# Two more feature tiles made and turned in the spatial stage of a one-core gMLP and linear-attention kernel

## The chip, the cores and the metric

The kernel runs on one core of a Trainium2 chip. Its engines are TensorE (PE, with its weight loads as PEld), VectorE (DVE), ScalarE (ACT), GpSimd (POOL) and the sync engine (SP), each with an instruction queue of its own. The time is device microseconds of one execution. Some runs are profiled: one execution with start and duration of each instruction.

## The reference

All is f32, S = 2048 rows, D = 512. The normalized input goes through two branches, which are added to x.

```python
xn = layernorm(x)
# branch A: 32 heads of 16, hedgehog features, linear attention
q, k, v = split(xn @ wqkv)
phi = concat(softmax(h @ w_phi), softmax(-h @ w_phi))     # for q and for k, per head
num = phi_q @ (phi_k.T @ v)
den = phi_q @ sum(phi_k) + 1e-6
A = (num / den) @ wo
# branch B: gMLP, Fh = 688
z = gelu(xn @ w_in);  z1 = z[:, :688];  z2 = layernorm(z[:, 688:])
g = w_sp @ z2 + b_sp[:, None]                             # w_sp is 2048 x 2048
B = (z1 * g) @ w_out
out = x + A + B
```

## The kernel before

Rows are handled in 16 tiles of 128. Products that need f32 accuracy are done with operands split in two, a part rounded to the PE's format and the remainder: `mm3` (lines 55 to 59) issues three matmuls for each, rounded by rounded (L57), rounded by remainder (L58), remainder by rounded (L59). ACT rounds (L49), DVE subtracts to get the remainder (L53).

The stages follow one another on PE. First come layer norm and the projections to k, v and q; the exponentials of the 16 tiles of q features and the reciprocals of their softmax sums go to DRAM as `e_d`. Then come the projections z1 (raw to DRAM, `z_d`) and z2 (gelu, layer norm, split into the B operands).

The **spatial stage** computes g = w_sp @ z2 for eight pairs of row tiles. It does so with the seven products P1 to P7 of a 2 x 2 scheme of Strassen's kind (`FORM`), whose A operands are A11, A22 and sums S1 to S4 of quarters of w_sp. A pair has four units (quarters of the columns); unit n is 42 matmuls on g. For each unit `load_a` fetches a raw tile wf on SP, and `prep_a` makes the operands: ACT rounds A11/A12, A22, S2/S1, S4/S3, and DVE makes four sums (L637 to L640) and four remainders (L53, `A<-wf,A`). This is done two units ahead, into two sets of tiles in turn. The raw tiles wf lie in a ring of three (f, x, y).

After a pair's last unit, DVE and ACT **drain** the seven products from PSUM into tile c (one ACT copy, seven DVE instructions, L834 to L840). Then `gate` multiplies: POOL has loaded the pair's z1 into tile z1t (L808), ACT takes its gelu (L850), DVE multiplies it with c (L853), and `turn` transposes the result in blocks of 32 on DVE (L862, L864) back into z1t. From there stores on SP bring it to DRAM in turned order (`u_d`, `ur_d`). Tiles c and z1t have one buffer each.

**Features** of q still need the denominator: `q_fin` (L563 to L570) multiplies with `zb`, the sums of phi_k, reduces, and scales; its operands are the tile's e and r from `e_d`. Tiles 0 and 1 are finished so before the spatial stage and stored back. After pairs 2 and 4 they are loaded into tile c by POOL (L967), turned by DVE (`turn_q`, L579) into tile z1t, and stored by POOL as `q_d` (L581). Tile 2 is finished at the end of the spatial stage, tiles 3 to 15 in the final stage (`features`).

The **final stage** goes over pairs of row tiles: `project_u` multiplies u with w_out, `attend` the turned features with kvT (po, L1062), `project_o` with wo. Features reach `attend` turned in two ways (`attend_T`): tile pair 0 and tiles from TQ = 8 on come from `q_d`; tiles 2 to 7 are transposed on PE (ptq, L1047) and copied by ACT. `ahead(i)` loads e of tile i + 5 and finishes tile i + 3.

The order on each engine is set by a scheduler, which places instructions by a timeline of its own and keeps each engine's queue in that order. At the border between the z2 projections and the spatial stage the function `in_turn` fixes, by a list of keys, the order of preparations, B splits and drain steps on DVE (first instruction of a key) and ACT (second).

Of the kernel before, what the change touches and what calls it, by code (L numbers as in the profile page):

```python
# [10 lines left out]
F32 = mybir.dt.float32  # L11
# [7 lines left out]
P = 128  # L19
# [22 lines left out]
def mixer(ctx: ExitStack, tc: tile.TileContext, x, x_t, wv, wqkT, phi_bd, wo, w_in, wst, b_r, w_out, out):  # L42
# [509 lines left out]

    QW = NF + 7 * H

    def load_q(s, et):
        sp.dma_start(et[:, :NF + 2 * H], e_d[s])
        return et

    def q_fin(et, tmp, zb):
# [40 lines left out]

    def load_a(n):
        i, q = SEQ[n]
        tag = "fx"[n] if n < 2 else "fxy"[(n - 2) % 3]
        t = (fy[0] if tag == "y" else ws).tile([P, 2, QC, P], F32, tag="wf" + tag, name="wf")
        for k in range(2):
            with tc.issue_after(load_a.last) if n == 5 else ExitStack():
                load_a.last = sp.dma_start(t[:, k], wst[2 * i + k, :, q * QC:(q + 1) * QC, :]).ins
        return [t[:, k].rearrange("p (k two) t -> p two k t", two=2) for k in range(2)]
# [37 lines left out]

    def in_turn(*keys):
        for e in range(2):
            queue = [turns[k][e] for k in keys if e < len(turns[k])]
            for a, b in zip(queue, queue[1:]):  # L650
                tc.add_manual_dep(b, a.name, mybir.DependencyInfo(
                    mybir.DependencyClass.NoSync, mybir.DependencyReason.DATA), reason="order of the border")
# [177 lines left out]
    def drain(i, g, cb):  # L830
        g = {k: t[:, :FC] for k, t in g.items()}
        b1, b2 = (bias[:, 2 * i + k:2 * i + k + 1] for k in range(2))
        c11, c12, c21, c22 = (cb[:, k, j] for k in range(2) for j in range(2))
        add = lambda o, p, b, q: dve.scalar_tensor_tensor(o, p, b, q, op0=ALU.add, op1=ALU.add)  # L834
        first = act.activation(c12, g["P1"], AF.Copy)
        steps = [add(c11, g["P2"], b1, c12),
                 dve.tensor_tensor(c21, g["P6"], c12, op=ALU.add),
                 dve.tensor_tensor(c12, g["P5"], c21, op=ALU.add),
                 add(c22, g["P7"], b2, c12),
                 dve.tensor_tensor(c21, g["P7"], c21, op=ALU.add),  # L840
                 add(c12, g["P3"], b1, c12)]
        drained = add(c21, g["P4"], b2, c21)
        for k, x in enumerate(steps + [drained]):
            turns["c", i, k] = x.ins,
        return cb, first.ins, drained.ins

    def gate(i, cb, z, u, ut, after=None):
        cb, first, _ = cb
        with tc.issue_after(after or first):
            act.activation(z[:, :, :FH], z[:, :, :FH], AF.Gelu_apprx_tanh)  # L850
        zs = z[:, :, :FH].rearrange("p k (j f) -> p k j f", j=2)
        us = u[:, :, :FH].rearrange("p k (j f) -> p k j f", j=2)
        dve.tensor_tensor(us, zs, cb, op=ALU.mult)  # L853
        lo, hi = u[:, :, KF * P:FH], u[:, :, FH:FU].bitcast(F32R)
        dve.tensor_copy(hi, lo)
        rest_l(lo, lo, hi)

        def turn():
            src = ut.rearrange("p k f -> p (k f)")
            m, r = src[:, :2 * KF * P], src[:, 2 * KF * P:]  # L860
            for k in range(2):
                dve.transpose(m[:, k * KF * P:(k + 1) * KF * P].rearrange("p (m c t) -> p m c t", c=KF, t=BL),  # L862
                              u[:, k, :KF * P].rearrange("p (c m j) -> p m c j", c=KF, j=BL))
            dve.transpose(r.rearrange("p (k f) -> p k f", k=2), u[:, :, KF * P:])  # L864
            eng = pool if i == NP - 2 else sp
            for b in range(0, P, BL):
                w = b // BL * KF * BL
                eng.dma_start(u_d[2 * i:2 * i + 2, :, w:w + KF * BL].rearrange("k (m j) w -> j (k m) w", j=BL),
                              m[b:b + BL].rearrange("p (m w) -> p m w", w=KF * BL))
                eng.dma_start(ur_d[2 * i:2 * i + 2, :, b:b + BL].rearrange("k (a j) t -> j (k a) t", j=BL),  # L870
                              r[b:b + BL].rearrange("p (a t) -> p a t", t=BL))

        return turn
# [44 lines left out]
    for n in range(NC):  # L918
        i = SEQ[n][0]
        if n % NQ == 1 and i < NP - 1:  # L920
            z = load_z1(i)
        if n:
            products(n, g)
        if n % NQ == NQ - 1 and i < NP - 1:
            c = gt.tile([P, 2, FU], F32, tag="c", name="c")
            cq = c[:, :, :FH].rearrange("p k (j f) -> p k j f", j=2)
            cb = drain(i, g, cq)
            g = {}
        if n + 4 < NC:
            raw[n + 4] = load_a(n + 4)  # L930
        if 0 < n < NC - 2:
            A[n + 2] = prep_a(n + 2, raw.pop(n + 2))
        if n == 6:
            in_turn((1, "sums"),
# [24 lines left out]
        if n % NQ == NQ - 1 and i < NP - 1:  # L959
            turn = gate(i, cb, z, c, z, prep_a.last)  # L960
            if i < NP - 2:
                turn()
            if i in (2, 4):
                s = i // 2 - 1
                e, t = (gt.tile([P, 2, FU], F32, tag=tag, name=name).rearrange("p k f -> p (k f)")[:, :NF]
                        for tag, name in (("c", "c"), ("z1", "z1t")))
                pool.dma_start(e, e_d[s, :, :NF])  # L967
                turn_q(s, t, e, pool)
        if n == NC - 4:
            stage_w()  # L970
        if n == NC - 3:
            zb = slot("zb")[:, :NF]
            sp.dma_start(zb, zb_d)
            uT = [first_gate(0)]
            ets[2] = load_q(2, slot("et"))
            es[2], last = q_fin(ets.pop(2), slot("qtmp")[:, :NF], zb)
        if n == NC - 2:
            fq = [slot("f")[:, :NF].rearrange("p (k b c t) -> p k b c t", k=2, c=NB // 2, t=BL) for h in range(2)]
            for k in range(2):
                for h in range(2):  # L980
                    sp.dma_start(fq[h][:, k], q_d[k].rearrange("p (b h w) -> h p b w", h=2, w=QB // 2)[h])
            t = xz_tile((KF + 1) * P, F32R, "u1")
            us = {1: load_u(1, t[:, :KF * P].bitcast(F32), t[:2 * REM, KF * P:(KF + 1) * P])}
    cb = drain(NP - 1, g, slot("c").rearrange("p (k j f) -> p k j f", k=2, j=2))
    with tc.issue_after(cb[2]):
        turn()
# [134 lines left out]
            rows = [(m * QP, (m + 1) * QP) for m in range(c // 2 * 8 + c % 2, (c // 2 + 1) * 8, 2)]  # L1121
            load_w(wo, rows, wo_h[:, c], wo_l[:, c], cw.tile([P, D], F32, tag="wof", bufs=4, name="wof"))
    with tc.issue_after(load_w.last):
        ets[3] = load_q(3, slot("et"))
        for s in (2, 3):
            us[s] = fetch_u(s)
        ets[4] = load_q(4, slot("et"))

    def ahead(i):

        if i + 5 < NT:
            ets[i + 5] = load_q(i + 5, slot("et"))
        if i + 4 < NT:
            with tc.issue_after(brought[i + 2]) if i + 6 >= NT else ExitStack():
                us[i + 4] = fetch_u(i + 4)
        if 3 < i + 3 < NT:
            features(i + 3)

    p, nxt = {}, dict(enumerate(uT))
    for i in range(0, NT, 2):  # L1140
# [10 lines left out]
            p[i + 1] = project_u(i + 1, u, q)  # L1151
        if not i:
            fin.append(lasts[7])
            features(3)
            with tc.issue_after(fin[-1]), tc.issue_after(lasts[8]):
                nxt[2] = gated(us.pop(2))
        if i < NT - 2:
# [48 lines left out]
```

## Time and profile before

| | us |
|---|---|
| median of 3 runs | 610.74 |
| lowest and highest | 610.21, 615.73 |
| profiled execution | 612.24 |
| its span, first to last instruction | 610.5 |
| granted PE clock | 1.000 |
| spatial stage, first g matmul to first pout matmul | 275.4 to 484.3 |

Times in the profile count from the start of the span. A row of a timeline gives start, length, engine, line, operation, what it writes and reads, how many instructions are merged and, in brackets, how long the engine stood idle before and what ended that. A row of the groups gives busy time and mean length in ns, then idle time before and its releasers. A row of waits gives who waited for whom: total, times, longest. The chain of waits is followed back from the last instruction. A releaser with a DMA's name is inferred from a semaphore that several transfers share, so the name can be that of another transfer.

### The profile page before, as it was taken

The page shows a single profiled execution, that of the slowest core. Times are in us where ns is not written, and L with a number is a line of the kernel's source. Part 1 is how long each engine was busy: PE and PEld are TensorE (multiplying, and loading weights), DVE is VectorE, ACT ScalarE, POOL GpSimd, SP SyncE. Part 2 cuts the span into 40 slices and gives each one's busy share as a digit, 9 for nine tenths or more (in the row PEclk, how much of TensorE's full clock was granted, in tenths as well). Part 3 has the DMA queues.
Part 4 walks back from the last instruction along what each step waited for, and adds up shares of the span by engine and source line. Part 5 has one row for each costly group of instructions (what it writes and reads, how often), then busy time and mean ns, then how long its engine had stood idle before and what let it go on. Part 6 is the DMA issues. An engine that isn't in the chain of part 4 may idle for free.

```text
span 610.5 us, 11382 instructions
## 1 busy us (share of the span) xinstructions
PE 602.8 (99%) x4286; PEld 548.5 (90%) x4286; DVE 525.4 (86%) x930; ACT 260.3 (43%) x414; POOL 131.8 (22%) x231
## 2 busy tenths in 40 slices
PE   8999999999999999999999999999999999999997
PEld 7888888888888999999999999999999988877775
DVE  5999999999987578989999897997998999999922
ACT  5643324423433547877434433443435343332220
POOL 4122332323111005442000001001100041153420
PEclk9999999999999999999999999999999999999999
DMA  8557876566537758002344736556664799699782
GB/s 315 193 130 178 217 176 188 145 168 165 144 96 221 241 201 306 5 1 65 121 107 135 208 104 173 163 154 161 176 185 154 228 299 292 191 326 248 183 236 67
DMA packets 57950, 107.85 MB, mean 177 GB/s; under 512 B 12392, under 2 KB 24552, under 8 KB 57672
## 3 DMA queue, kind: packets, MB, share of 16 engines
q1 hardware_dynamic: 43656, 65.22, 34.6%
q0 software_dynamic: 11936, 36.28, 24.2%
q10 hardware_dynamic: 2304, 5.64, 2.4%
q8 instruction: 33, 0.54, 0.4%
q14 instruction: 21, 0.17, 0.1%
HBM read 66.85 MB, written 35.54 MB: 168 GB/s over the span
## 4 chain that ended last, share of the span: by engine, by line
PE 82%; DVE 5%; ACT 4%; issue 4%; POOL 3%; DMA 1%; ACTq 0%; POOLq 0%; DVEq 0%
PE g L57 9%; PE g L59 9%; PE g L58 9%; PE proj L58 7%; PE proj L57 7%; PE proj L59 7%; PE pout L57 5%; PE pout L59 5%; PE pout L58 5%; PE zps L57 3%; PE zps L59 3%; PE zps L58 3%; PE po L1062 1%; DMA et<-e_d 1%; PE kvps L372 1%
## 5 line engine op out<-in xcount | busy, mean ns | idle before, releaser
L57 PE MATMUL g<-B,A 128*128 128x344 f32 x448 | 140.4, 317 | 0.9 <-ACT A L49 0.9
L58 PE MATMUL g<-B,A 128*128 128x344 f32 x448 | 141.1, 317 | 0.0
L59 PE MATMUL g<-B,A 128*128 128x344 f32 x448 | 135.5, 317 | 0.0
L49 ACT ACTIVATE A<-wf 128x512 fp32r<-128x512 f32 (+1 forms) x128 | 69.9, 573 | 109.5 <-DVE wf L639 64.8
L57 PEld LDWEIGHTS g<-B,A 128*128 128x128 f32 x448 | 83.8, 188 | 1.4 <-ACT A L49 1.4
L53 DVE TENSOR_TENSOR A<-wf,A 128x512 fp32r<-128x512 f32 (+1 forms) x128 | 76.5, 619 | 9.8 <-ACT A L49 9.4
L58 PEld LDWEIGHTS g<-B,A 128*128 128x128 f32 x448 | 84.0, 188 | 0.0
L59 PEld LDWEIGHTS g<-B,A 128*128 128x128 f32 x448 | 82.7, 188 | 0.3 <-DVE A L53 0.2
L57 PE MATMUL proj<-wqk_h,xT 128*128 128x512 f32 x128 | 50.1, 391 | 0.0
L59 PE MATMUL proj<-wqk_h,xT 128*128 128x512 f32 x128 | 49.8, 389 | 0.0
L58 PE MATMUL proj<-wqk_l,xT 128*128 128x512 f32 x128 | 49.8, 389 | 0.0
L124 ACT ACTIVATE e<-e,r_x 128x1024 f32<-128x1024 f32 x26 | 29.7, 1148 | 42.2 <-DVE e L123 41.2
L57 PE MATMUL zps<-w1h,xT 128*128 128x344 f32 (+2 forms) x128 | 40.9, 320 | 0.0
L59 PE MATMUL zps<-w1h,xT 128*128 128x344 f32 (+2 forms) x128 | 40.7, 318 | 0.0
L58 PE MATMUL zps<-w1l,xT 128*128 128x344 f32 (+2 forms) x128 | 40.7, 318 | 0.0
L57 PE MATMUL zps<-w2h,xT 128*128 128x344 f32 (+2 forms) x128 | 40.7, 318 | 0.0
L58 PE MATMUL zps<-w2l,xT 128*128 128x344 f32 (+2 forms) x128 | 40.6, 317 | 0.0
L59 PE MATMUL zps<-w2h,xT 128*128 128x344 f32 (+2 forms) x128 | 40.3, 317 | 0.0
L127 DVE TENSOR_REDUCE sm<-e 128x64 f32<-128x1024 f32 x26 | 31.1, 1199 | 2.5 <-ACT e L124 2.5
L808 POOL DMA_DIRECT2D z1t<-z_d x16 | 9.1, 594 | 105.3 <-DVE A L53 38.2
L57 PE MATMUL pout<-wu,uh 128*128 128x512 f32 x75 | 30.4, 406 | 0.0
L59 PE MATMUL pout<-wu,ul 128*128 128x512 f32 x75 | 29.3, 391 | 0.0
(217 smaller groups left out, 1373.0 us busy)
## 6 DMA issues: line engine op xcount, KB each, us to landing
wf<-in_wst SPq DMA_DIRECT2D x64, 256.0 KB, 3.8
e_d<-e POOLq DMA_DIRECT2D x16, 544.0 KB, 4.4
et<-e_d SPq DMA_DIRECT2D x16, 544.0 KB, 7.1
z_d<-z1f ACTq DMA_DIRECT2D x16, 344.0 KB, 2.9
z1t<-z_d POOLq DMA_DIRECT2D x16, 344.0 KB, 4.2
zacc<-e POOLq DMA_DIRECT2D x10, 512.0 KB, 4.8
u<-u_d SPq DMA_DIRECT2D x15, 320.0 KB, 4.9
xt<-in_x SPq DMA_DIRECT2D x16, 256.0 KB, 4.3
```

What stands on the lines that cost most here:

```text
L49: return act.activation(h, src, AF.Copy).ins
L53: return (eng or dve).tensor_tensor(l, src, h.bitcast(F32), op=ALU.subtract).ins
L57: pe.matmul(dst, ah, bh, start=start, stop=False)
L58: pe.matmul(dst, ah, bl, start=False, stop=False)
L59: return pe.matmul(dst, al, bh, start=False, stop=stop).ins
L124: softmax_pair.last = less, act.activation(e, e, AF.Exp, scale=scale).ins
L127: dve.tensor_reduce(sm, heads(e), axis=AX.X, op=ALU.add)
L372: i = pe.matmul(kv_acc[k:k + QP, m // 4], vs[:, m * QP:(m + 1) * QP], e[:, m * HP:(m + 1) * HP], start=first and m < 4 and len(ready) == n ...
L808: pool.dma_start(t[:, k, :FH], z1_d[2 * i + k])
L1062: lasts[3] = pe.matmul(po[r][c * QP:(c + 1) * QP, k], kvT[rows, m // 2, cols], fs[m // 4][rows, m // 2 % 2], start=True, stop=True).ins
```

## The change

Tiles 2 and 3 are now finished in the spatial stage: after pairs 1 to 4 tiles 2, 0, 3, 1 are loaded into c by POOL, and 2 and 3 go through `q_fin` there, with `zb` loaded into a tile zs that takes the place of the third raw tile (y) from unit 8 on. All four are turned and stored. In the final stage pair 1 loads its turned features (`ft[2]`), tile 4 takes the place of tile 2 at the end of the spatial stage, and `ahead(i)` finishes tile i + 5 and loads e of tile i + 7. The list at the border gets the ACT copy of drain 0, the gelu, the product and the transposes of gate 0, and for units 8 to 31 all preparations keep one fixed order.

```diff
-    def load_q(s, et):
-        sp.dma_start(et[:, :NF + 2 * H], e_d[s])
+    def load_q(s, et, eng=None):
+        (eng or sp).dma_start(et[:, :NF + 2 * H], e_d[s])
...
-        tag = "fx"[n] if n < 2 else "fxy"[(n - 2) % 3]
+        tag = "fx"[n] if n < 2 else "fxy"[(n - 2) % 3] if n < 8 else "fx"[n % 2]
...
-        if n + 4 < NC:
+        if n < 6:
             raw[n + 4] = load_a(n + 4)
         if 0 < n < NC - 2:
             A[n + 2] = prep_a(n + 2, raw.pop(n + 2))
+        if 6 <= n < NC - 4:
+            raw[n + 4] = load_a(n + 4)
+        if n == 6:
+            zs = fy[0].tile([P, 2, QC, P], F32, tag="wfy", name="zs").rearrange("p a b c -> p (a b c)")
+            pool.dma_start(zs, zb_d)
...
-                    (6, "A11"), (6, "A22"), (6, "first"), (6, "sums"), (6, "S2"), (6, "S4"),
+                    (6, "A11"), (6, "A22"), ("z", 0), (6, "first"), (6, "sums"), (6, "S2"), (6, "S4"),
+                    ("u", 0),
...
-            if i in (2, 4):
-                s = i // 2 - 1
-                e, t = (gt.tile([P, 2, FU], F32, tag=tag, name=name).rearrange("p k f -> p (k f)")[:, :NF]
+            if 0 < i < 5:
+                s = (2, 0, 3, 1)[i - 1]
+                e, t = (gt.tile([P, 2, FU], F32, tag=tag, name=name).rearrange("p k f -> p (k f)")
                         for tag, name in (("c", "c"), ("z1", "z1t")))
-                pool.dma_start(e, e_d[s, :, :NF])
+                t = t[:, :NF]
+                if s < NE:
+                    e = e[:, :NF]
+                    pool.dma_start(e, e_d[s, :, :NF])
+                else:
+                    e, _ = q_fin(load_q(s, e[:, :QW], pool), t, zs)
                 turn_q(s, t, e, pool)
...
-            ets[2] = load_q(2, slot("et"))
-            es[2], last = q_fin(ets.pop(2), slot("qtmp")[:, :NF], zb)
+            ets[4] = load_q(4, slot("et"))
+            es[4], last = q_fin(ets.pop(4), slot("qtmp")[:, :NF], zb)
...
+    in_turn(*((n, k) for n in range(8, NC) for k in ("A11", "A22", "first", "sums", "S2", "S4")))
...
-        ets[3] = load_q(3, slot("et"))
-        for s in (2, 3):
-            us[s] = fetch_u(s)
-        ets[4] = load_q(4, slot("et"))
+        ets[5] = load_q(5, slot("et"))
+        us[2] = fetch_u(2)
+        ft[2] = f_pair()
+        for k in range(2):
+            sp.dma_start(ft[2][:, k], q_d[2 + k])
+        us[3] = fetch_u(3)
+        ets[6] = load_q(6, slot("et"))
...
-        if i + 5 < NT:
-            ets[i + 5] = load_q(i + 5, slot("et"))
+        if i + 7 < NT:
+            ets[i + 7] = load_q(i + 7, slot("et"))
         if i + 4 < NT:
-            with tc.issue_after(brought[i + 2]) if i + 6 >= NT else ExitStack():
+            with tc.issue_after(brought[i + 4]) if i + 6 >= NT else ExitStack():
                 us[i + 4] = fetch_u(i + 4)
-        if 3 < i + 3 < NT:
-            features(i + 3)
+        if 0 < i < NT - 5:
+            features(i + 5)
```

Three places show what moves. The first is DVE's queue at gate 0: the end of the preparation of unit 6 and that of unit 7. Before:

```order
L53 TENSOR_TENSOR A<-wf,A 128x2x256 x2
L853 TENSOR_TENSOR c<-z1t,c 128x2x688
L53 TENSOR_TENSOR A<-wf,A 128x2x256
L53 TENSOR_TENSOR A<-wf,A 128x256
L855 CAST c<-c 128x2x48
L862 STREAM_TRANSPOSE z1t<-c 128x640 x2
L637 TENSOR_TENSOR wf<-wf 128x2x128
```

After:

```order
L53 TENSOR_TENSOR A<-wf,A 128x2x256 x2
L854 TENSOR_TENSOR c<-z1t,c 128x2x688
L53 TENSOR_TENSOR A<-wf,A 128x2x256
L53 TENSOR_TENSOR A<-wf,A 128x256
L856 CAST c<-c 128x2x48
L637 TENSOR_TENSOR wf<-wf 128x2x128
L53 TENSOR_TENSOR c<-c 128x2x48
L638 TENSOR_TENSOR wf<-wf 128x2x128
L866 STREAM_TRANSPOSE z1t<-c 128x192
L639 TENSOR_TENSOR wf<-wf 128x2x128
L640 TENSOR_TENSOR wf<-wf 128x2x128
L53 TENSOR_TENSOR A<-wf,A 128x2x256 x2
```

The product of gate 0 stood after the preparation of unit 5 and stands one unit later now, and the two large transposes follow only behind the whole preparation of unit 7.

The second is DVE's queue after pair 1's gate, from its last transpose on (units 10 and 11). Before:

```order
L864 STREAM_TRANSPOSE z1t<-c 128x192
L639 TENSOR_TENSOR wf<-wf 128x2x128
L640 TENSOR_TENSOR wf<-wf 128x2x128
L53 TENSOR_TENSOR A<-wf,A 128x2x256 x2
L53 TENSOR_TENSOR A<-wf,A 128x256
L637 TENSOR_TENSOR wf<-wf 128x2x128
```

After (c is now the tile of loaded features, zs the sums of phi_k):

```order
L866 STREAM_TRANSPOSE z1t<-c 128x192
L639 TENSOR_TENSOR wf<-wf 128x2x128
L640 TENSOR_TENSOR wf<-wf 128x2x128
L53 TENSOR_TENSOR A<-wf,A 128x2x256 x3
L53 TENSOR_TENSOR A<-wf,A 128x256
L637 TENSOR_TENSOR wf<-wf 128x2x128
L638 TENSOR_TENSOR wf<-wf 128x2x128
L563 TENSOR_TENSOR z1t<-c,zs 128x1024
L639 TENSOR_TENSOR wf<-wf 128x2x128
L564 TENSOR_REDUCE c<-z1t 128x64
L640 TENSOR_TENSOR wf<-wf 128x2x128
```

Eight instructions of preparations stand between the last transpose and L563; the rest of the normalization and L579 are spread through the preparations of units 11 and 12.

The third is POOL's queue in the spatial stage. Before:

```order
L808 DMA z1t<-z_d 128x688 x6
L967 DMA c<-e_d 128x1024
L581 DMA q_d<-z1t 32x4x256 x4
L808 DMA z1t<-z_d 128x688 x4
L967 DMA c<-e_d 128x1024
```

After:

```order
L808 DMA z1t<-z_d 128x688 x2
L939 DMA zs<-zb_d 128x1024
L808 DMA z1t<-z_d 128x688 x2
L556 DMA c<-e_d 128x1088
L581 DMA q_d<-z1t 32x4x256 x4
L808 DMA z1t<-z_d 128x688 x2
L979 DMA c<-e_d 128x1024
L581 DMA q_d<-z1t 32x4x256 x4
L808 DMA z1t<-z_d 128x688 x2
```

Every load of z1 from pair 2 to pair 5 now stands behind a feature load and four feature stores; before, only those of pairs 3 and 5 did.

More of the change, by code (lines that the diff above doesn't have):

```diff
@@ L648, in in_turn @@
         for e in range(2):
-            queue = [turns[k][e] for k in keys if e < len(turns[k])]
+            queue = [turns[k][e] for k in keys if e < len(turns[k]) and turns[k][e]]
             for a, b in zip(queue, queue[1:]):
@@ L844, in drain @@
             turns["c", i, k] = x.ins,
+        turns["c12", i] = None, first.ins
         return cb, first.ins, drained.ins
@@ L849, in gate @@
         with tc.issue_after(after or first):
-            act.activation(z[:, :, :FH], z[:, :, :FH], AF.Gelu_apprx_tanh)
+            turns["z", i] = None, act.activation(z[:, :, :FH], z[:, :, :FH], AF.Gelu_apprx_tanh).ins
         zs = z[:, :, :FH].rearrange("p k (j f) -> p k j f", j=2)
         us = u[:, :, :FH].rearrange("p k (j f) -> p k j f", j=2)
-        dve.tensor_tensor(us, zs, cb, op=ALU.mult)
+        turns["u", i] = dve.tensor_tensor(us, zs, cb, op=ALU.mult).ins,
         lo, hi = u[:, :, KF * P:FH], u[:, :, FH:FU].bitcast(F32R)
@@ L861, in turn @@
             for k in range(2):
-                dve.transpose(m[:, k * KF * P:(k + 1) * KF * P].rearrange("p (m c t) -> p m c t", c=KF, t=BL),
-                              u[:, k, :KF * P].rearrange("p (c m j) -> p m c j", c=KF, j=BL))
+                turns["ut", i, k] = dve.transpose(
+                    m[:, k * KF * P:(k + 1) * KF * P].rearrange("p (m c t) -> p m c t", c=KF, t=BL),
+                    u[:, k, :KF * P].rearrange("p (c m j) -> p m c j", c=KF, j=BL)).ins,
             dve.transpose(r.rearrange("p (k f) -> p k f", k=2), u[:, :, KF * P:])
@@ L945, in mixer @@
                     (3, "S4"),
[1 row of a table removed]
+                    (4, "A11"), (4, "A22"), ("c12", 0), (4, "first"), (4, "sums"),
                     ("c", 0, 0),
@@ L955, in mixer @@
                     (5, "first"), (5, "sums"), (5, "S2"), (5, "S4"),
[1 row of a table removed]
+                    (6, "A11"), (6, "A22"), ("z", 0), (6, "first"), (6, "sums"), (6, "S2"), (6, "S4"),
+                    ("u", 0),
                     (7, "A11"), (7, "A22"), (7, "first"), (7, "sums"), (7, "S2"), (7, "S4"),
+                    ("ut", 0, 0), ("ut", 0, 1),
                     (8, "A11"), (8, "A22"), (8, "first"), (8, "sums"), (8, "S2"), (8, "S4"))
@@ L1153, in mixer @@
             fin.append(lasts[7])
-            features(3)
+            features(5)
             with tc.issue_after(fin[-1]), tc.issue_after(lasts[8]):
```

1 row of the table g is left out of this document.

## Prediction

> **What bounds the kernel now.** I read the page's busy table first, then busy time by stage, then the vector engine's timeline where it stands still, and last the chain of waits for the final stage.
>
> ```profile
> PE 602.8 (99%) x4286; PEld 548.5 (90%) x4286; DVE 525.4 (86%) x930; ACT 260.3 (43%) x414; POOL 131.8 (22%) x231
> ...
> 326.50:378.10 51.60, 51.60 (x337) 51.55 (x336) 43.93 (x91) 20.62 (x35) 3.81 (x7) 1.00 0.52 147
> 378.10:429.70 51.60, 51.60 (x337) 51.60 (x336) 45.45 (x94) 20.64 (x36) 4.90 (x9) 1.00 0.58 161
> 429.70:481.30 51.60, 51.60 (x337) 51.60 (x336) 46.17 (x91) 23.31 (x40) 2.16 (x4) 1.00 0.63 188
> sum 154.80, PE 154.80 PEld 154.75 DVE 135.55 ACT 64.57 POOL 10.88; mean PE 51.60 PEld 51.58 DVE 45.18 ACT 21.52 POOL 3.63
> ```
>
> The lower rows are the spatial stage by stretches of two pairs (eight units): length, then busy time of PE, PEld, DVE, ACT and POOL, then granted clock, DMA share, GB/s. PE never stops and its clock is full, so whatever keeps PE fed there is free, and whatever doesn't is added to the time. DVE is idle for 154.80 - 135.55 = 19.25 us of this stage. What that idle time is decides the forecast:
>
> ```profile
> 365.38 0.37 DVE L864 STREAM_TRANSPOSE z1t<-c 128x192 f32<-128x192 f32 x1
> ...
> 366.76 1.29 DVE L53 TENSOR_TENSOR A<-wf,A 128x512 fp32r<-128x512 f32 x2 [0.24 <-ACT A L49]
> 368.33 0.43 DVE L53 TENSOR_TENSOR A<-wf,A 128x256 fp32r<-128x256 f32 x1 [0.28 <-ACT A L49]
> ...
> 373.03 1.25 DVE L579 STREAM_TRANSPOSE z1t<-c 128x1024 f32<-128x1024 f32 x1 [3.36 <-DMA wf<-in_wst]
> ...
> 375.44 0.69 DVE L53 TENSOR_TENSOR A<-wf,A 128x512 fp32r<-128x512 f32 x1
> 376.24 0.36 PE L59 MATMUL g<-B,A 128*128 128x344 f32 x1
> ...
> 417.22 0.37 DVE L864 STREAM_TRANSPOSE z1t<-c 128x192 f32<-128x192 f32 x1
> 424.02 1.25 DVE L579 STREAM_TRANSPOSE z1t<-c 128x1024 f32<-128x1024 f32 x1 [2.50 <-DMA wf<-in_wst]
> ...
> DVE z1t L579 <- DMA wf<-in_wst: 5.9, 2, 3.4
> DVE c L853 <- ACT z1t L850: 3.2, 6, 0.6
> DVE c L834 <- PE g L59: 0.9, 2, 0.7
> DVE c L837 <- PE g L59: 0.3, 1, 0.3
> ```
>
> Of the 19.25 us, 5.9 are two waits in which L579 (turning a feature tile) stands at the head of DVE for its DMAs while ready work queues behind it. 3.2 are waits of the gate's product for ACT's gelu. Only 0.9 + 0.3 us are waits for PE, the sign of a DVE that has run ahead as far as it may. The remaining 9.0 us are mostly pieces of about 0.3 us, as at 366.76, in which a remainder waits for ACT to round. So DVE isn't waiting for PE: the two run neck and neck. The row at 375.44 shows it. It is S2's remainder for unit 15, done at 376.13, and the matmul that reads it (the third of its group) starts at 376.24: after one L579 and its wait, 0.1 us of lead is left. TensorE is at its limit here and DVE has no lead to give.
>
> [...]
>
> **The change, part by part.**
>
> Removed on PE: 16 transposes for pair 1, since its features now come turned. Also the stall before pair 12, if features run two tiles ahead:
>
> ```profile
> 498.76 1.75 PE ptq L1047 x16
> 581.84 0.45 PE L1062 MATMUL po<-f,kvT 64*32 64x256 f32 x8 [1.06 <-issue]
> 303.54 0.39 PE L57 MATMUL g<-B,A 128*128 128x344 f32 x1 [0.25 <-ACT A L49]
> 318.52 0.43 PE L57 MATMUL g<-B,A 128*128 128x344 f32 x1 [0.64 <-ACT A L49]
> ```
>
> PE sets the pace of the final stage, so this is -1.75 and -1.06 us. The four ACT copies of the transposes go too; ACT isn't the bound, so they count nothing. The fixed orders at the border aim at the two stalls of 0.25 and 0.64: -0.9 us. They don't remove DVE work there, they put the transposes of pair 0 later, so they gain no more than that; at worst nothing.
>
> Added on DVE in the spatial stage: for tiles 2 and 3 each a normalization (L563 to L570) and a turn (L579).
>
> ```profile
> 493.75 1.23 DVE L563 TENSOR_TENSOR qtmp<-et,zb 128x1024 f32<-128x1024 f32 x1 [0.39 <-DMA et<-e_d]
> ...
> 497.39 1.23 DVE L570 TENSOR_TENSOR et<-et 128x1024 f32<-128x1024 f32 x1
> 498.54 1.55 DVE L53 TENSOR_TENSOR ul<-u,uh 128x640 fp32r<-128x640 f32 x2
> ```
>
> One normalization runs from 493.75 to the next start at 498.54: 4.8 us; with 1.25 for L579 that is 6.05, and 12.1 for both. They stand between other work in the new order and may use the pieces of idle time. Of the 9.0 us of pieces plus 1.2 for PE I give half, 5.1. Net +7.0; ends +1.9 (all 10.2 filled) and +12.1 (nothing filled).
>
> Added wait at L563. Like L579 before, L563 needs the load of the features into tile c (which may start only after L864, renumbered L866) and the stores of the turned u, whose tile z1t it overwrites. Before, the two L579 started 7.3 and 6.4 us after L864 ended (373.03 - 365.75, 424.02 - 417.59), 6.8 in the mean. In the new order there stand, between that transpose and L563, two sums, the remainders of S2 and S4, then A11 and A22 of unit 11 (19) and two sums. By the rows of one preparation:
>
> ```profile
> 320.76 0.43 DVE L637 TENSOR_TENSOR wf<-wf 128x256 f32<-128x256 f32 x1
> ...
> 322.88 2.23 DVE L53 TENSOR_TENSOR A<-wf,A 128x512 fp32r<-128x512 f32 x4 [0.32 <-ACT A L49]
> ```
>
> four sums and the four remainders take 322.88 + 2.15 - 320.76 = 4.27 us, and just these eight stand there: 4.3. So 6.8 - 4.3 = 2.5 us of standing still, twice: +5.0; ends 0 (the load lands early or DVE is busy longer) and 6.0. The L579 of tiles 0 and 1 keep their waits.
>
> Added wait at the gate's product (L853, now L854). After L579 the z1t tile is stored by POOL, and only then may POOL load the next pair's z1 into it; ACT's gelu and the product follow.
>
> ```profile
> 374.57 2.22 POOL L581 DMA_DIRECT2D q_d<-z1t  x4 [7.66 <-DVE wf L639]
> 381.28 1.10 POOL L808 DMA_DIRECT2D z1t<-z_d  x2 [4.50 <-DMA wf<-in_wst]
> ...
> z1t<-z_d POOLq DMA_DIRECT2D x16, 344.0 KB, 4.2
> ...
> 387.12 1.34 ACT L850 ACTIVATE z1t<-z1t 128x1376 f32<-128x1376 f32 x1
> ...
> L834 DVE SCALAR_TENSOR_TENSOR c<-g,bias,c 128x344 f32<-128x344 f32 x32 | 18.0, 572 | 1.7 <-PE g L59 0.9 <-ACT A L49 0.2
> L837 DVE TENSOR_TENSOR c<-g,c 128x344 f32<-128x344 f32 x8 | 4.1, 511 | 0.3 <-PE g L59 0.3
> ```
>
> From the end of L579 (374.28) to the second of the two load issues (381.28 + 0.55), its landing (4.2) and the gelu (1.34) is 13.1 us; with 0.2 for two hand-overs, 13.3. Before, this ran twice; now it runs four times, with less work in it. In the new order the DVE work between L579 and the next product is, for pair 1: the rest of preparation 12 (1.8), a drain of seven (4 x 0.57 + 3 x 0.51 = 3.8), a whole preparation (4.27) and four more instructions (1.95), less 0.08 for each of 14 that start while the one before still ends (four remainders last 2.48 singly and 2.23 in a row): 10.7. Counted alike the later three have 11.9, 11.1 and 12.0. That leaves waits of 2.6, 1.4, 2.2 and 1.3, together 7.5. Each product waited about 0.5 for its gelu before (3.2 over six), so 7.5 - 2.0 = +5.5; ends 0 and 7.5.
>
> The other loads and stores: POOL issues two feature loads of 544 KB, one of zb and two sets of four stores more; it is busy 3.81 of 51.6 us there and the DMA share is 0.52 to 0.63. These I cost at nothing. The wf ring has two tiles in place of three from unit 8 on, so a load waits for the preparation two units back, and has the one between to land in: at least 4.27 us, and a product of the gate or a drain beside it in nearly every unit, against 3.8 us to landing by the page's median for wf. Nothing; without that cover some 0.5 us for a unit that has nothing else. On SP the loads of pair 1's turned features stand ahead of u of tile 3; they are needed only some 10 us later, nothing. The final stage loses two normalizations on DVE, which isn't its bound: nothing beyond the 1.06.
>
> Since DVE has no lead to spend, its sum lengthens the stage: 7.0 + 5.0 + 5.5 = +17.5. Then -0.9 (border) - 1.75 - 1.06: +13.8 us. The profiled execution took 612.24 us (span 610.5), so 626.0 by it; it lies 1.5 above the median of 610.74, so 624.5 for the median.
>
> **Rivals.**
>
> *All of it is hidden.* If the 19.25 us of idle DVE time could be used freely, the 12.1 us of new work would vanish in them: -1.75 - 1.06, with up to -0.9, ends at 607 to 608. It decides if L563 finds its data there and leads are larger than at unit 15. For it: 88% busy DVE against a full PE. Against it: only 1.2 us of that idle time were spent waiting for PE. [...]
>
> *DVE is the bound, but z1 arrives in time.* If DVE does other waiting between L579 and the product, the 13.3 us are covered: +8.3, 619.
>
> *Only the work counts.* Both waits are covered, 7.0 - 3.7 = +3.3: 614, within 1%.
>
> *Worse.* Nothing is filled and all waits are at their upper ends: 12.1 + 6.0 + 7.5 - 2.8 = +22.8: 633.5.
>
> **How the numbers follow.** About 1%, 6.1 us, is what a measurement of this kernel can tell from no change. The forecast (620 to 630) has 0.45, z1 in time (616 to 620) 0.17, only the work (610 to 616) 0.15, hidden (604 to 610) 0.18, worse 0.05. Slower by over 1% (above 616.9): the forecast, worse and nearly all of 619, 0.66. Within 1%: only the work and most of hidden, 0.30. Faster by over 1% (below 604.6): 0.04, since the gains found add up to 3.7 us. The likeliest is 624.5. The range takes in the hidden case at its lower end and most of the forecast: 608 to 630; the forecast's own is 620 to 630.
>
> **What would show it.** Right: PE idle or late before g matmuls in units 12 to 31, ended by A from DVE or ACT; DVE gaps of 2 to 3 us before L563 and of 1 to 3 us before L854; no stall before pair 12; 32 transposes of ptq; a spatial stage some 16 us longer. Wrong: a spatial stage of the old length, no gap at L563 or L854, or a po that waits for pair 1's features.

## The result, and the profile after

| | before | changed |
|---|---|---|
| median, 5 runs each | 611.35 | 635.95 |
| lowest and highest | 610.21, 615.73 | 633.65, 638.61 |
| profiled execution, its span | 612.24, 610.5 | 638.61, 636.9 |
| spatial stage, first g matmul to first pout | 208.8 | 234.8 |
| from the first pout to the end | 126.3 | 125.9 |

The changed kernel is slower: ratio 1.0391, 95% interval 1.0357 to 1.0424, 24.6 us where 13.8 were forecast, and outside the range of 608 to 630. The profiled executions differ by 26.4 us: 26.0 of them lie in the spatial stage, 0.9 ahead of it, and the final stage gained 0.5 of the 2.8 us that were forecast.

The first block below is the busy line of the page after. The second is the stage from unit 8 to the first pout in one window, first of before, then of after (length, busy time of PE, PEld, DVE, ACT and POOL, granted clock, DMA share, GB/s).

```profile
PE 613.4 (96%) x4270; PEld 553.2 (87%) x4270; DVE 526.6 (83%) x932; ACT 255.4 (40%) x410; POOL 137.9 (22%) x242
```

```profile
328.80:484.30 155.50, 155.50 (x1011) 155.45 (x1010) 136.44 (x275) 65.31 (x112) 10.88 (x20) 1.00 0.58 165
```

```profile
328.00:511.10 183.10, 167.31 (x1011) 162.15 (x1010) 148.14 (x295) 64.76 (x116) 17.56 (x32) 0.96 0.56 161
```

The same 1011 matmuls take 27.6 us longer (units 0 to 7 take 1.6 less). DVE has 11.7 us more work (148.14 - 136.44), about the 12.1 that were computed. But its idle time did not fill up; it grew from 19.1 to 35.0 us. Whatever made the stage longer made DVE wait too. What it waited for, in the waits of the spatial stage after:

```profile
DVE A L53 <- ACT A L49: 13.7, 16, 4.2
DVE c L854 <- ACT z1t L851: 8.0, 6, 4.5
DVE z1t L563 <- DMA wf<-in_wst: 6.0, 2, 3.4
DVE z1t L579 <- DMA wf<-in_wst: 2.8, 1, 2.8
```

The last three are the waits that the prediction named: the gate's product (L854, before L853) for its gelu, and the features (L563, L579) for their loads and stores. The first is a wait for ACT's rounding of the raw tiles. Its growth was costed at nothing; before it was 5.0 us in 20 pieces of at most 0.4. Where in the stage the time went is best read from the starts of the gate's product, one for each pair from pair 1 to pair 6. In DVE's timeline of before:

```profile
335.26 1.58 DVE L853 TENSOR_TENSOR c<-z1t,c 128x1376 f32<-128x1376 f32 x1
360.52 1.59 DVE L853 TENSOR_TENSOR c<-z1t,c 128x1376 f32<-128x1376 f32 x1 [0.56 <-ACT z1t L850]
388.50 1.59 DVE L853 TENSOR_TENSOR c<-z1t,c 128x1376 f32<-128x1376 f32 x1 [0.47 <-ACT z1t L850]
412.36 1.59 DVE L853 TENSOR_TENSOR c<-z1t,c 128x1376 f32<-128x1376 f32 x1 [0.55 <-ACT z1t L850]
439.63 1.59 DVE L853 TENSOR_TENSOR c<-z1t,c 128x1376 f32<-128x1376 f32 x1 [0.62 <-ACT z1t L850]
464.11 1.59 DVE L853 TENSOR_TENSOR c<-z1t,c 128x1376 f32<-128x1376 f32 x1 [0.55 <-ACT z1t L850]
```

And of after:

```profile
336.27 1.59 DVE L854 TENSOR_TENSOR c<-z1t,c 128x1376 f32<-128x1376 f32 x1 [0.46 <-ACT z1t L851]
369.98 1.59 DVE L854 TENSOR_TENSOR c<-z1t,c 128x1376 f32<-128x1376 f32 x1 [0.77 <-ACT z1t L851]
399.43 1.59 DVE L854 TENSOR_TENSOR c<-z1t,c 128x1376 f32<-128x1376 f32 x1 [4.45 <-ACT z1t L851]
434.16 1.59 DVE L854 TENSOR_TENSOR c<-z1t,c 128x1376 f32<-128x1376 f32 x1 [1.67 <-ACT z1t L851]
462.78 1.59 DVE L854 TENSOR_TENSOR c<-z1t,c 128x1376 f32<-128x1376 f32 x1 [0.22 <-ACT z1t L851]
488.86 1.59 DVE L854 TENSOR_TENSOR c<-z1t,c 128x1376 f32<-128x1376 f32 x1 [0.47 <-ACT z1t L851]
```

From one product to the next, PE has four units to do, 4 x 6.45 = 25.8 us (eight took 51.60 before). Before, the five steps are 25.3, 28.0, 23.9, 27.3 and 24.5, together 128.9, or five times 25.8 within 0.2: the pairs with a feature (2 and 4) are too long, and the others make it good. After, they are 33.7, 29.5, 34.7, 28.6 and 26.1: none is shorter than PE's time, nothing is made good.

What fills 33.7 us in pair 1? These rows are of DVE's, POOL's and ACT's timelines of after:

```profile
341.12 0.37 DVE L866 STREAM_TRANSPOSE z1t<-c 128x192 f32<-128x192 f32 x1
348.29 1.22 DVE L563 TENSOR_TENSOR z1t<-c,zs 128x1024 f32<-128x1024 f32 x1 [2.55 <-DMA wf<-in_wst]
356.21 1.24 DVE L579 STREAM_TRANSPOSE z1t<-c 128x1024 f32<-128x1024 f32 x1
```

```profile
342.12 0.54 POOL L556 DMA_DIRECT2D c<-e_d  x1 [11.81 <-DVE wf L639]
357.74 2.23 POOL L581 DMA_DIRECT2D q_d<-z1t  x4 [15.09 <-DVE z1t L579]
364.00 1.11 POOL L808 DMA_DIRECT2D z1t<-z_d  x2 [4.02 <-DMA wf<-in_wst]
```

```profile
368.59 1.35 ACT L851 ACTIVATE z1t<-z1t 128x1376 f32<-128x1376 f32 x1 [0.76 <-DMA z1t<-z_d]
```

One tile, z1t, goes through all of it: product (336.27), turned until 341.5, stored to DRAM, overwritten by L563 at 348.3, by L579 until 357.5, stored again, loaded with the next z1 from 364.0 on, ready for the gelu at 368.6, next product at 370.0. This **round trip** of z1t is 33.7 us long, 7.9 us over PE's time, and the chain of waits of after follows it here: from the transposes over their stores to L563, through the normalization, over a DMA to the load of z1, the gelu and the product. But the trip runs in part through DVE's queue, and DVE is busy for 28.4 of the 33.7 us; its product then stood for only 0.77 us until the gelu was done. So the trace of this pair alone doesn't separate two theories. Theory 1, that of the prediction: DVE's work and waits add up. Theory 3: the round trip sets the length of such a pair, and where DVE waits meanwhile is secondary. (Theory 2, in between, blamed the two raw tiles.) Slower DMAs are not the reason: from issue to landing the page gives z1's loads 4.2 us before and 4.0 after, and the DMA share from unit 8 on is 0.58 before and 0.56 after.

### The profile page after: what moved, and what is told of

It reads as the page before. It is cut to its first block, busy times and chain, and to the rows that moved or that the text cites. A ratio compares the mean times of both kernels' runs of the same rounds, so it can differ in the third digit from the quotient of the medians.

```text
span 636.9 us, 11390 instructions
## 1 busy us (share of the span) xinstructions
PE 613.4 (96%) x4270; PEld 553.2 (87%) x4270; DVE 526.6 (83%) x932; ACT 255.4 (40%) x410; POOL 137.9 (22%) x242
## 3 DMA queue, kind: packets, MB, share of 16 engines
q0 software_dynamic: 12752, 38.97, 24.7%
## 4 chain that ended last, share of the span: by engine, by line
PE 65%; DVE 13%; DMA 13%; issue 4%; ACT 2%; SPq 2%; POOL 0%; DVEq 0%; ACTq 0%; POOLq 0%
PE proj L58 7%; PE proj L57 7%; PE proj L59 7%; PE zps L57 6%; PE zps L59 6%; PE zps L58 6%; PE g L57 5%; PE g L58 5%; PE g L59 5%; DMA wf<-in_wst 3%; PE pout L59 3%; PE pout L57 3%; PE pout L58 3%; DVE A L53 2%; DMA et<-e_d 2%
## 5 line engine op out<-in xcount | busy, mean ns | idle before, releaser
L57 PE MATMUL g<-B,A 128*128 128x344 f32 x448 | 145.3, 327 | 14.2 <-ACT A L49 10.6
L49 ACT ACTIVATE A<-wf 128x512 fp32r<-128x512 f32 (+1 forms) x128 | 66.7, 569 | 124.7 <-DVE wf L639 101.5
L57 PEld LDWEIGHTS g<-B,A 128*128 128x128 f32 x448 | 86.2, 193 | 18.0 <-ACT A L49 13.4
L53 DVE TENSOR_TENSOR A<-wf,A 128x512 fp32r<-128x512 f32 (+1 forms) x128 | 74.2, 617 | 17.7 <-ACT A L49 17.6
L58 PEld LDWEIGHTS g<-B,A 128*128 128x128 f32 x448 | 86.6, 193 | 0.0
L59 PEld LDWEIGHTS g<-B,A 128*128 128x128 f32 x448 | 82.4, 192 | 2.9 <-DVE A L53 2.9
L127 DVE TENSOR_REDUCE sm<-e 128x64 f32<-128x1024 f32 x26 | 31.1, 1199 | 2.5 <-ACT e L124 2.5
L57 PE MATMUL pout<-wu,uh 128*128 128x512 f32 x75 | 30.5, 406 | 0.0
L58 PE MATMUL pout<-wu,uh 128*128 128x512 f32 x75 | 29.2, 390 | 0.0
```

The source lines that it names most:

```text
L49: return act.activation(h, src, AF.Copy).ins
L53: return (eng or dve).tensor_tensor(l, src, h.bitcast(F32), op=ALU.subtract).ins
L57: pe.matmul(dst, ah, bh, start=start, stop=False)
L58: pe.matmul(dst, ah, bl, start=False, stop=False)
L59: return pe.matmul(dst, al, bh, start=False, stop=stop).ins
L127: dve.tensor_reduce(sm, heads(e), axis=AX.X, op=ALU.add)
```

## The experiments

A first set asked what the added work costs and whether two raw tiles are to blame. **no_fin** leaves the normalization out:

```diff
-                if s < NE:
+                if s < NE or s in (2, 3):
```

> The changed kernel, with tiles 2 and 3 loaded, turned and stored in the spatial stage but not normalized (L563 to L570 left out, so pair 1's features lack their denominators). All loads, stores, rings and fixed orders stay. The changed kernel took 636 us. Theory 1 (the vector engine is the bound of the spatial stage, so its work counts in full): about 2 x 4.8 us less, 624 to 628, with the waits for raw tiles (about 10 us) still there. Rival (the added work was hidden and only waits count): 633 to 637.

Measured: 622.07, ratio 1.0175 (1.0148 to 1.0201). Leaving out 9.6 us of DVE work saved 13.9, more than all of it. The waits for raw tiles went too (A L53 from 13.7 to 6.6 us), which Theory 1 had not expected. The normalization did more than take DVE's time. And 10.6 us of loss are left with no normalization in the stage and with z1 in time (the product's waits are 2.8 us over six pairs).

**no_fin3** is no_fin with the ring `"fxy"[(n - 2) % 3]` and the loads' place restored.

> As no_fin (normalization of tiles 2 and 3 left out), but with three raw tiles and the loads issued ahead of the preparation, as before the change; zb's sums are not loaded. Theory 1 (two raw tiles make the loads of w_sp late, about 10 us of DVE waiting for ACT's rounding, which waits for the raw tile): 7 to 10 us below no_fin, 615 to 620. Rival (raw tiles are late only because the vector engine is late; the ring is innocent): within 2 us of no_fin.

Measured: 623.08 (1.0203, 1.0166 to 1.0240), no different from no_fin. Here the ring is innocent.

**ring2** is the kernel before with the new ring, and with the loads issued behind the preparation as in the change (the second part isn't shown here):

```diff
-        tag = "fx"[n] if n < 2 else "fxy"[(n - 2) % 3]
+        tag = "fx"[n] if n < 2 else "fxy"[(n - 2) % 3] if n < 8 else "fx"[n % 2]
```

> The kernel before with one edit: two raw tiles in place of three from unit 8 on, loads of a unit n + 4 issued after the preparation of unit n + 2. Nothing else of the change. Theory 1 (the ring has a price of its own): slower by 3 to 9 us, 614 to 620, with DVE waits for ACT's rounding of 1 us and more, which end with a raw tile's landing. Rival (ring innocent): 610 to 612.

Measured: 621.23 (1.0153, 1.0135 to 1.0171), 9.7 us slower. So in the kernel before the ring and the later loads do have a price, and "nothing" was wrong there. Nine waits of ACT's rounding were of 0.9 to 2.4 us.

**no_order** is the changed kernel without the fixed order of units 8 to 31.

> The changed kernel without the fixed order of the preparations of units 8 to 31 (the border's list stays). Theory 1 (work, waits at features, raw tiles): 633 to 638, no change beyond what the scheduler's own order moves by chance. Rival (the fixed order is what makes the raw tiles and the products wait): 8 us or more faster, 628 or below.

Measured: 638.52 (1.0435, 1.0404 to 1.0466). The fixed order isn't what costs.

The second set put the ring and the round trip to the test in the changed kernel itself. **fin3** gives it three raw tiles and the loads' place again, as no_fin3 did. The tile zs has no room then, so L563 multiplies e with itself, the same instruction on other data:

```diff
-                    e, _ = q_fin(load_q(s, e[:, :QW], pool), t, zs)
+                    e, _ = q_fin(load_q(s, e[:, :QW], pool), t, e[:, :NF])
```

> The changed kernel with three raw tiles throughout and the loads issued ahead of the preparation, as before the change. For that, the tile of the sums of phi_k goes: in the spatial stage q_fin of tiles 2 and 3 multiplies e with itself in its place (same instructions, same sizes; the denominators of pair 1 are not the reference's). All features, turns and fixed orders stay. Theory 2 (once the vector engine has more to do, late raw tiles of a two-tile ring cost about 10 us of the 636): 624 to 629, and no wait of ACT's rounding for a raw tile above 1 us. Rival (as no_fin against no_fin3 suggests, the ring costs nothing; the waits would come up elsewhere): 633 to 637.

Measured: 636.43 (1.0417, 1.0387 to 1.0447): no gain. Its waits tell why:

```profile
DVE c L854 <- ACT z1t L851: 11.0, 6, 4.4
DVE z1t L579 <- DMA wf<-in_wst: 7.3, 2, 4.3
DVE z1t L563 <- DMA wf<-in_wst: 7.1, 2, 3.7
DVE A L53 <- ACT A L49: 3.5, 11, 0.3
```

The waits for raw tiles are gone (13.7 to 3.5 us), and those at the product (8.0 to 11.0), L579 (2.8 to 7.3) and L563 (6.0 to 7.1) have taken their place: 30.5 in the changed kernel, 28.9 here. DVE gets sooner to a tile that isn't there. Waits that only change their name don't set the time.

**own_t** takes z1t out of the features' way: the features are turned into the place of the third raw tile, and e is multiplied with itself as in fin3 (L563 takes 1.23 us so, 1.22 in the changed kernel).

```diff
-                t = t[:, :NF]
+                t = fy[0].tile([P, 2, QC, P], F32, tag="wfy", name="t").rearrange("p a b c -> p (a b c)")
```

> The changed kernel with two raw tiles, but the turned features of tiles 2, 0, 3, 1 go into a tile of their own (the place of the third raw tile) and not into z1t; q_fin multiplies e with itself in place of the sums, as in fin3. So the next pair's z1 need not wait for the features' stores, and L563 not for the stores of the turned u. Theory 1 (z1 late at the gate's product costs about 5 us, part of the waits at L563 and L579 too): 625 to 631, the product's waits for gelu down from 8.0 to about 3. Rival (these waits only take the place of waits for raw tiles): 633 to 637.

Measured: 630.04 (1.0311, 1.0269 to 1.0353), 5.9 us faster than the changed kernel, the product's waits 2.8 as forecast. The steps of pairs 1 and 3 fall to 30.9 and 31.1, no further. Its waits:

```profile
DVE t L579 <- DMA c<-e_d: 6.2, 2, 3.2
DVE A L53 <- ACT A L49: 6.2, 15, 1.7
DVE t L563 <- DMA c<-e_d: 5.4, 2, 2.9
DVE c L854 <- ACT z1t L851: 2.8, 6, 0.5
```

The features' own waits (L563, L579) are still there, 11.6 us in all, although the features no longer need z1t; the expectation that they fall too did not hold. In pair 1 DVE is busy for 26.9 of the 30.9 us, so with the trip out of the way DVE's own queue, its work and its waits, is still 5 us longer than PE's time. The trip is not all of the loss: without it 5.9 of the 24.6 us are gone.

**store_late** was to move SP's stores of the turned u behind a raw tile's load.

> The changed kernel with the stores of the turned u on SP placed behind the load of a raw tile that they stood ahead of (pairs 1 to 5). Theory 2b (a raw tile's load waits in SP's queue behind up to eight stores that wait for the transposes): the waits of ACT's rounding for raw tiles fall from 10 to about 4 us, the z1 and feature waits rise by less: 630 to 634. Rival (the ring alone delays the loads): 635 to 638 or slower, since the stores are later and free z1t later.

Its edit moved no instruction on any queue, so 634.15 (1.0380, 1.0348 to 1.0412) is a second reading of the changed kernel (634.15 against 635.95 shows how far two sets of runs differ), and the question about SP's order stays untried. The rows that raised it, SP's and DVE's of the changed kernel, were these: half a raw tile's load behind four stores, and DVE 4.16 us without work.

```profile
440.60 0.63 SPq L607 DMA_DIRECT2D wf<-in_wst  x1
441.27 3.42 SPq L872 DMA_DIRECT2D ur_d<-z1t  x4
444.73 1.42 SPq L607 DMA_DIRECT2D wf<-in_wst  x3
```

```profile
447.72 0.69 DVE L53 TENSOR_TENSOR A<-wf,A 128x512 fp32r<-128x512 f32 x1 [4.16 <-ACT A L49]
```

The third set separates work from round trip. **chain3** is the kernel before with a long round trip and no DVE work:

```diff
+            if i in (1, 3):
+                for k in range(3):
+                    t = gt.tile([P, 2, FU], F32, tag="z1", name="z1t").rearrange("p k f -> p (k f)")[:, :NF]
+                    pool.dma_start(t, e_d[8 + k, :, :NF])
```

> The kernel before with nothing added on the vector engine: after pairs 1 and 3 POOL loads three feature tiles, one after the other, into z1t (what they bring is overwritten by the next z1 and never read), so that pair 2's and pair 4's z1 come late, as behind the features of tiles 2 and 3 in the changed kernel (there it landed 32 and 33 us after the gate's product of the pair before). Theory 3 (the round trip of the one z1t tile, from one product to the next, sets the length of these pairs): z1 lands about 28 to 33 us after the product, these two pairs last 30 to 34 us in place of 25 and 24, slower by 6 to 14 us, 617 to 625. Rival, theory 1 (only the vector engine's own work counts): 610 to 613.

Measured: 625.01 (1.0214, 1.0186 to 1.0241), 13.6 us slower without a single instruction more on DVE, at the upper end of what was expected. The product of pair 2, and the gelu that it waits for:

```profile
334.91 1.58 DVE L853 TENSOR_TENSOR c<-z1t,c 128x1376 f32<-128x1376 f32 x1
368.81 1.59 DVE L853 TENSOR_TENSOR c<-z1t,c 128x1376 f32<-128x1376 f32 x1 [9.19 <-ACT z1t L850]
```

```profile
367.43 1.35 ACT L850 ACTIVATE z1t<-z1t 128x1376 f32<-128x1376 f32 x1 [8.53 <-DMA z1t<-z_d]
```

The gelu starts 32.5 us after the product before (in the changed kernel 368.59 - 336.27 = 32.3), and the step is 33.9 (there 33.7). A late z1 alone can make the pair that long.

**no_fin_work** goes the other way: DVE work on the base of no_fin, in no chain with z1t.

```diff
+            if n in (11, 12, 19, 20):
+                rest_l(l, src, h)
```

> The kernel no_fin (changed kernel, normalization of tiles 2 and 3 left out; 622 us) with the vector work put back in another form: in the preparations of units 11, 12, 19 and 20 each remainder is computed twice (16 more instructions of about 0.56 us, 9.0 us, against 9.6 us left out), in no chain with c or z1t. Theory 1 (the vector engine's work counts in full wherever it stands): 629 to 635. Theory 3 (the round trip of z1t through the normalization is what counts): 622 to 626.

Measured: 628.00 (1.0263, 1.0231 to 1.0295): 5.9 us for 9.0 us of work, between the two expectations. With z1 in time (the product's waits are 2.8 here too) work counts by two thirds.

**no_fin_chain** completes the square on that base: chain3's loads (two of them, behind the feature stores) in no_fin.

> The kernel no_fin (changed kernel, tiles 2 and 3 not normalized, 622 us) with the round trip made long again and no vector work: behind the feature stores of pairs 1 and 3 POOL loads two feature tiles, one after the other, into z1t (never read). It completes a square: neither work nor a long round trip 622, work alone (no_fin_work) 628, both (the changed kernel) 636. Theory 3 (the round trip of z1t sets the length of pairs 1 and 3): z1 lands about 32 us after the product, these pairs last 32 to 34 us, 630 to 635. Rival (what is missing from 628 to 636 is vector work, not the round trip): 622 to 626.

Measured: 641.45 (1.0485, 1.0461 to 1.0509), slower even than the changed kernel and 6 us above the range expected. Pairs 1 and 3 do become the long ones, but the gelu starts 34.0 and 36.6 us after the product before, not about 32, and the scheduler put the product behind more preparations (DVE is busy for 28.8 us of pair 1's step, for 23.0 in no_fin, and for less in the steps behind). So the size isn't the trip's alone. All runs of this kind side by side, the steps from product to product read as above:

| kernel | median | pair 1 | 2 | 3 | 4 | 5 |
|---|---|---|---|---|---|---|
| before | 611.35 | 25.3 | 28.0 | 23.9 | 27.3 | 24.5 |
| no_fin: neither | 622.07 | 27.0 | 27.6 | 27.9 | 27.9 | 25.2 |
| no_fin_work: work | 628.00 | 31.6 | 27.5 | 32.3 | 28.0 | 25.4 |
| no_fin_chain: round trip | 641.45 | 35.4 | 29.0 | 38.0 | 28.8 | 25.0 |
| changed: both | 635.95 | 33.7 | 29.5 | 34.7 | 28.6 | 26.1 |
| store_late: the changed kernel again | 634.15 | 33.8 | 27.2 | 34.7 | 28.3 | 24.6 |
| no_fin3: neither, three raw tiles | 623.08 | 27.8 | 27.5 | 28.2 | 28.3 | 24.7 |
| chain3: round trip, on before | 625.01 | 33.9 | 26.6 | 32.6 | 27.3 | 23.8 |
| own_t: work, short trip | 630.04 | 30.9 | 27.7 | 31.1 | 28.7 | 25.5 |

Work alone gives 5.9 us, a long round trip alone 19.4, the normalization 13.9. The square doesn't show whether work and trip add, because the trip that was tried alone is longer than that of the changed kernel (steps of 35.4 and 38.0 against 33.7 and 34.7). own_t, which has the work and not the trip, splits the loss better. Four turned features, the new orders and the new final stage cost 10.6 us (no_fin against before), the normalization with z1t out of its way 8.0 more (own_t against no_fin), and its passage through z1t another 5.9 (the changed kernel against own_t).

Two more runs were for the small terms. **border** is the kernel before with the longer list at the border.

> The kernel before with the border's longer list alone (ACT copy of drain 0, gelu, product and transposes of gate 0). As predicted: the two stalls before units 4 and 6 go, 0.9 us faster, 609.5 to 611. Rival (the scheduler's order behind the border gets worse): 612 to 616.

Measured: 610.85 (0.9995, 0.9982 to 1.0007), no change that can be told. The two stalls do go, and in the one profile the stage is 0.9 us shorter (207.9).

**final_only** takes the spatial additions away and keeps the new final stage:

```diff
-            if 0 < i < 5:
-                s = (2, 0, 3, 1)[i - 1]
+            if i in (2, 4):
+                s = i // 2 - 1
...
-            sp.dma_start(ft[2][:, k], q_d[2 + k])
+            sp.dma_start(ft[2][:, k], q_d[k])
```

> The changed kernel without its additions in the spatial stage: only tiles 0 and 1 turned there, after pairs 2 and 4, three raw tiles, no fixed order of units 8 to 31; the border's list and the new final stage stay. Pair 1 loads the turned features of pair 0, which stand in DRAM, in place of its own. As predicted (PE loses 16 transposes, 1.75 us, and the stall before pair 12, 1.06 us; border 0 to 0.9): 607 to 609. Rival (the two normalizations of one pair, issued together, make PE wait about as much in the final stage, as in the profile after): 610 to 612.

Measured: 613.36 (1.0030, 1.0015 to 1.0045), slower by 2.0 us where 3.7 less were forecast, and above both expectations. Its profile shows one stall of PE of 2.6 us at 499, behind u of tile 3, which SP loads after the features. **u3_first** loads it ahead of them.

> The kernel final_only (613.4 us) with one change of order on SP: in the final stage u of tile 3 is loaded ahead of pair 1's two feature loads of 512 KB, not behind them. Theory (u of tile 3 lands late, ACT's rounding of it stands at the head of ACT ahead of the copies that free the PSUM tiles of pair 0, and PE waits 2.6 us): that stall goes, 610 to 611.5. Rival (something else delays ACT there): 613 to 614.

Measured: 613.76 (1.0032, 1.0015 to 1.0049). That stall went as expected, the time did not: PE now waits 1.42 and 0.40 us for remainders of oT. The order on SP isn't what holds the final stage's gain back.

## Why the prediction was wrong

The direction and the features' waits at L563 were right; the amount was 11 us short. Two steps failed. The gains of 3.7 us did not come, and the idle pieces of DVE were hardly filled. Here are the terms against the profiled execution, with before's own steps (in the list above) as the base. store_late is the same program, so it is a second reading.

| term | forecast | changed, 638.61 us | store_late, 632.80 us |
|---|---|---|---|
| pairs 1 and 3: work, L563, product | +15.8 (7.0 + 5.0 + 2.6 + 2.2 - 1.0) | +19.3 (68.4 - 49.1) | +19.4 |
| pairs 2 and 4: product | +1.7 (1.4 + 1.3 - 1.0) | +2.8 (58.1 - 55.3) | +0.2 |
| pair 5 | 0 | +1.6 | +0.1 |
| last product to first pout | 0 | +2.1 (22.2 against 20.1) | +0.6 |
| border, to the first product of the list above | -0.9 | +0.1 | +0.1 |
| final stage | -2.8 | -0.5 | -0.7 |
| before the stage | 0 | +0.9 | +0.8 |
| sum | +13.8 | +26.3 | +20.5 |

Both readings share two things: pairs 1 and 3 took some 3.5 us more than forecast, and the gains did not come. The rest (pairs 2, 4 and 5 and the end of the stage) is 6.5 us in one execution and 0.9 in the other, of one program, against the forecast's 1.7; no missing term can be read from it.

- **The gains (-0.9 - 1.75 - 1.06 = -3.7).** This is the step that failed most. final_only has the border's list and the new final stage without the additions in the spatial stage, and it is 2.0 us slower than before: 5.7 of the 10.8 us that the forecast was short, by the medians. (By the two profiles of the changed kernel these terms, with the time before the stage, come to +0.5 and +0.2, about 4 us short.) no_fin bears it out: by the forecast's terms it should have cost 2.5 + 5.0 - 3.7 = 3.8 us (two turns, two waits, the gains) and it cost 10.6. In its profile the five steps took 6.7 us more, near the 7.5, but the part from the first pout on took 128.9 us, 2.6 more and not 2.8 less. The transposes went (ptq from 48 to 32) and the stall before pair 12 too, but a new stall stands in its place: 1.57 us in the changed kernel, 2.60 in final_only. From the first pout to the end the kernels here that have the new final stage took 125.2 to 130.0 us, those with the old one 124.9 to 126.3. The forecast took an engine's removed work and a removed stall as time gained, without asking what PE waits for next. In the final stage after, the stall is for a remainder that stands on DVE behind a turn and a part of a normalization:

```profile
567.58 1.24 DVE L579 STREAM_TRANSPOSE qtmp<-et 128x1024 f32<-128x1024 f32 x1
568.74 1.17 DVE L564 TENSOR_REDUCE et<-qtmp 128x64 f32<-128x1024 f32 x1
569.83 1.27 DVE L53 TENSOR_TENSOR oT<-po,oT 128x512 fp32r<-128x512 f32 x2
```

```profile
570.56 0.50 PE L59 MATMUL pout<-woh,oT 128*128 128x512 f32 x1 [1.57 <-DVE oT L53]
```

- **Work (+7.0 net).** This is the second step that failed. The two normalizations are 9.6 us of work, and less 5.1 us of filled idle time they were to cost 4.5. With z1t out of their way they cost 8.0 (own_t against no_fin), so of the idle pieces at most some 1.6 us were filled. The work in no_fin_work was cheaper, 5.9 for 9.0. The 3.5 us that pairs 1 and 3 took beyond the forecast in both readings are as much as this difference, though they are not shown to be the same.
- **L563 (+5.0).** Right: 2.55 and 3.40 us, together 6.0, in store_late 6.3.
- **Gate's product (+5.5).** The sum was right: own_t, which removes the late z1, is 5.9 us faster, and the waits grew by 5.3 (8.0 - 2.7). The distribution wasn't: 0.8, 4.5, 1.7 and 0.2 in place of 2.6, 1.4, 2.2 and 1.3.
- **"DVE has no lead to give."** The lead of 0.1 us was read at unit 15, right behind a feature. The steps of before show that DVE falls back in pairs 2 and 4 (28.0 and 27.3 us against PE's 25.8) and makes it good in 1, 3 and 5. The change puts features into pairs 1 and 3, and in no_fin, where all four pairs have a turn alone, each takes 27.0 to 27.9, in no_fin3 27.5 to 28.3. This price was in the sum all the same: it is the 2.5 + 5.0 us that no_fin's steps bear out.
- **"Since DVE has no lead to spend, its sum lengthens the stage."** Not the whole mechanism: chain3 adds no DVE work and costs 13.6. The prediction had two pieces of the round trip (6.8 us to L563, 13.3 behind L579) but booked them as waits on DVE and never added up the trip: 5.2 from product to the end of the last turn, 6.8 to L563, about 9 through the normalization with the preparations between (9.2 after), 13.3 to the product, some 34, against 33.7 and 34.7. By the forecast's terms pairs 1 and 3 came to 49.1 + 15.8 = 64.9 us, 32.5 each. The trip would have shown that they need some 34, whatever DVE's idle pieces take up.
- **Ring of two raw tiles ("nothing").** With the later loads it costs 9.7 in the kernel before, so the argument was wrong; in the changed kernel and in no_fin three raw tiles gain nothing (fin3, no_fin3), so the sum did not suffer from it. That was luck.

Not settled are the 0.9 us before the stage (the first g matmul begins between 275.3 and 276.5 in the kernels run here), why final_only and u3_first do not come out below the kernel before, and how much of the loss is PE's clock (the last section). The rival "Worse" was the nearest (633.5), by a sum of upper ends and not by this account; that it came near is chance. The rival "hidden" is out: the idle time of DVE, 19.1 us before, was not room for the work and grew with it to 35.0.

## What to carry to other kernels

Where a tile has one buffer, follow it once around (written, stored, overwritten, stored, loaded, read) and add up that trip from the timeline. The stretch can't be shorter than the trip, so compare it with the time of the bounding engine; here they were 33.7 and 25.8 us. Then look at what is next behind it: with the trip out of the way the stretch was still 30.9 us, by DVE's queue. Test a forecast gain by itself: an engine relieved of work and of one wait may stand at the next one. And a wait that disappears in an experiment proves nothing until the time goes with it: here 10 us of waits for raw tiles changed their name and the kernel stayed at 636.

## What the hardware showed unexpectedly

PE's lost time in the stage is not all idle time. In PE's timeline after, a stall of 2.11 us is followed, 1.1 us later, by 13 matmuls at a start-to-start of about 0.287 us in place of 0.154, until 502.45, 3.7 us in all:

```profile
497.62 0.43 PE L57 MATMUL g<-B,A 128*128 128x344 f32 x1 [2.11 <-ACT A L49]
...
498.76 0.46 PE L59 MATMUL g<-B,A 128*128 128x344 f32 x1 [0.23 <-DVE A L53]
499.03 0.48 PE L57 MATMUL g<-B,A 128*128 128x344 f32 x1
499.31 0.49 PE L58 MATMUL g<-B,A 128*128 128x344 f32 x1
...
502.45 0.32 PE L58 MATMUL g<-B,A 128*128 128x344 f32 x1
502.61 0.32 PE L57 MATMUL g<-B,A 128*128 128x344 f32 x1
```

There are four such spells, near 359, 407, 455 and 499, of 11 to 13 matmuls each. All 47 took 13.4 us where 47 x 0.154 = 7.2 would do, 6.2 us more. The granted clock within them is 0.50, and its mean from unit 8 on is 0.96 where it was 1.00. Not every stall brings one: after 1.78 us at 420 none came (the granted clock is 1.00 from 422.04 to 426). In store_late, the same program, the stall at 358 is as long (1.78 us there, 1.77 in the changed kernel) and brought none; it has two spells in all (granted clock of the profiled execution 0.994, in the changed kernel 0.988). The spells last 3.2 to 3.7 us each. They begin 1.1 to 1.8 us after a stall of 1.73 to 2.11 us has ended, and 2.11 us is the longest idle time of PE in this stage; what sets them off is not shown. Nor is what they cost. From unit 8 on DVE waited for PE once, for 1.38 us until 506.00, behind the last spell, so a part may have fallen into time in which PE would have waited anyway. On the other hand no_fin, with 10.6 us of loss, has no spell in the stage (clock of its profiled execution 0.997), and own_t has two (0.992).
